# Two one-bank tiles in place of one two-bank tile for the transposes of an attention kernel, and own output banks for the MoE behind it

## Chip, cores and metric

One core of a Trainium2 chip runs the whole program. The metric is the device time of one execution, in microseconds, and its median over several runs. The profile shows one execution more. PE is TensorE (PEld its weight loads), ACT is ScalarE, DVE is VectorE, POOL is GpSimd, and SP issues most of the DMAs.

## What is computed

Attention over 4 batches of 8 heads, 576 positions and 64 values each, with a bias made by a small network from the log distance of two positions; then a feed-forward layer over the 2304 tokens, whose activation is a ratio of two polynomials ("MoE" in the code, though it has one expert). All is fp32.

```python
# attention
scores = q @ k.T / sqrt(64)
x = log1p(|i - j|) / log1p(max(i, 1))
scores += (relu(x * w1 + b1) @ w2)[head]        # 32 hidden units
attn = exp(scores - max(scores)); attn /= sum(attn) + 1e-9
out = attn @ v
# feed-forward, x is out with the heads side by side: 2304 x 512
h = x @ w_in                                    # 512 -> 2048
P = a0 + a1*h + a2*h**2 + a3*h**3
Q = 1 + |b0|*|h| + |b1|*h**2
y = (P / (Q + 1e-6)) @ w_out                    # 2048 -> 512
```

## The kernel before

The program has three stages in one hand-written order (`manual_schedule`): each engine executes its instructions in the order in which the code emits them, and the framework adds the waits on semaphores between engines. What an instruction waits for follows from the tiles that it reads and writes.

PSUM has eight banks of 512 fp32 columns. Before the change they are four tiles of two banks for the whole program: `HB[0]`, `HB[1]`, `HB[2]` and `TP`.

**Tables** (lines 640 to 735). The bias network is evaluated for 36 groups of 16 rows, in a fixed order. ACT and DVE make the hidden units (ring tiles, lines 684 and 686), PE multiplies by w2 (line 711) into `pa`, one of the four PSUM tiles in turn, and ACT evacuates it with a scale (line 716). The result goes to DRAM, and the bias tiles of the first pair of heads are read back from there. The units of row group y+2 are emitted ahead of the evacuation of y. The first two attention steps, `start(0)` and `start(1)`, are emitted behind the third-last and the last group.

**Attention** (lines 544 to 638). A step is 128 queries of a pair of heads; there are 72 steps (`NS`), and a round `rnd(r)` handles the steps i = 2r and i+1, with 35 rounds in the loop and the rest in `start` and `finish`. The scores of the two heads (j = 0, 1) go to `hb(i, j) = HB[(2i + j) % 3]`. PE works on the two halves of its rows (partitions 0 to 63 and 64 to 127) side by side; `weave` emits one list of operations for each half, by estimated times. In a round:
- first weave: scores of step i (line 329), and the transposes of the probabilities of step i-2 (line 413): sixteen of 64 x 64, eight by each half of PE. Half r writes `TP[:, r]`, its own bank. Two or more further ones ("ends") go to a spare part of a score tile.
- `copy(1)`, then `copy(0)` (line 430): ACT copies the bank of a half into the SBUF tile `pt`. Between the two stands another ACT operation, in many rounds a pass over expert weights (line 154).
- `tails` (line 433): DVE copies the ends. `e_ttr` (line 341): DVE adds bias to scores and finds the row's minimum. `e_exp` (line 357): ACT takes the exponential.
- second weave: scores of step i+1 and transposes of step i-1 into the same `TP`; then `copy(1)` and `copy(0)` again, with an exponential between.
- products with v (line 466) of steps i-3 and i-2, into spare parts of score tiles, copied out by DVE (line 476).

Beside this, DVE, ACT and POOL split the feed-forward weights into a high and a low part (lines 119 to 187), one job in three of four rounds.

`finish` transposes the last two steps with `copy()` for both banks at once, and starts the first products of the MoE.

**MoE** (lines 754 to 943). Ten passes: five token tiles (384 or 512 tokens) times two halves of the hidden units. A step s is two blocks of 128 hidden units: `mm1` (line 307) into `HB[s % 2]`, the ratio on ACT and DVE (`rat0`, `rat1`, `dvu` to `dv4`, `pl1`), and two steps later `mm2` (line 850) into the output banks, up to four of 128 tokens, kept over the four steps of a pass. `OUT` names them: the two banks of `TP` and of `HB[2]`. In the step after a pass `evac` copies them out (ACT, line 866, in the first five passes) or adds them to the first half's (DVE, line 871).

Of the kernel before, what the change touches and what calls it, by code (L numbers as in the profile page):

```python
# [16 lines left out]
P = 128  # L17
# [19 lines left out]
def tile_attn_moe(  # L37
# [53 lines left out]
    npool = ctx.enter_context(tc.tile_pool(name="npool", bufs=2))  # L91
    nc.gpsimd.memset(npool.tile([P, 64], F32, tag="fill", name="fill2", bufs=1)[:, 0:8], 0.0)
    psum = ctx.enter_context(tc.tile_pool(name="psum", bufs=1, space=PSUM))
    HB = [psum.tile([P, 2, 512], F32, tag=f"h{i}", name=f"hb{i}") for i in range(3)]
    TP = psum.tile([P, 2, 512], F32, tag="tp", name="tp")
    wsc = {}
    U16 = mybir.dt.uint16
    FN = KD * P
# [123 lines left out]
    with tc.manual_schedule():  # L222
# [3 lines left out]
        with ExitStack() as actx:  # L226
            apool = actx.enter_context(tc.tile_pool(name="apool", bufs=1))
            qkp = actx.enter_context(tc.tile_pool(name="qkp", bufs=2))
            epool = actx.enter_context(tc.tile_pool(name="epool", bufs=3))
            vpool = actx.enter_context(tc.tile_pool(name="vpool", bufs=3))  # L230

            sums = [apool.tile([P, P], F32, tag=f"sum{i}", name=f"sum{i}") for i in range(4)]
            for t in sums:
# [171 lines left out]
            def e_tp(i, sp, us):  # L405
                t = pt[i] = epool.tile([P, 9, P], F32, tag="pt", name=f"pt{i}")
                pb = prob.pop(i)
                ps = TP.rearrange("p r (x s) -> p r x s", s=64)
                to = t[:, 0:8].rearrange("p x (r s) -> p r x s", r=2)

                def turn(r, out, src):
                    x = slice(64 * r, 64 * r + 64)
                    T.transpose(out, src[x, :], ident[x, x])  # L413

                def op(*args):
                    return 57, lambda: turn(*args)

                main, ends = [], []
                for r in range(2):
                    main.append([  # L420
                        op(r, ps[:, r, x], pb[:, (S + 64 if x % 2 == 0 else 0) + x // 2 * P:][:, :P])
                        for x in range(8)
                    ])
                    ends.append([op(r, sp[:, r, SH:SH + 64], pb[:, 512:512 + P])])
                    for u in us:
                        ends[r].append(op(r, sp[:, r, SH + 64:SH + P], sums[u % 4]))

                def copy(r=None):
                    x = slice(0, 2) if r is None else r
                    A.copy(out=to[:, x], in_=ps[:, x])  # L430

                def tails():
                    op = V.tensor_copy(
                        out=t[:, 8].rearrange("p (r s) -> p r s", r=2), in_=sp[:, :, SH:SH + 64]
                    )
                    for u in us:
                        n = nsum(u)
                        rt = epool.tile([10, P], F32, tag="rt", name=f"rt{u}", bufs=2)
                        rsum[u] = dpool.tile([n, P], F32, tag=f"rs{u}", name=f"rs{u}")
                        V.tensor_copy(  # L440
                            out=rt[0:n].rearrange("p (r s) -> p r s", r=2), in_=sp[0:n, :, SH + 64:SH + P]
                        )
                        nc.sync.dma_start(out=rsum[u], in_=rt[0:n])
                    return op

                return main, ends, copy, tails
# [169 lines left out]
            def finish():  # L616
                run(puts)
                main, ends, copy, tails = turned(NS - 2, HB[2], ())
                weave(*(main[r] + ends[r] for r in range(2)))
                copy()  # L620
                tails()
                mm1(0, 0)
                recip(NS - 1)
                run(norms)
                main, ends, copy, tails = turned(NS - 1, HB[1], (NS - 1,))
                weave(*(main[r] + ends[r] for r in range(2)))
                copy()
                put = [e_pv(NS - 3, HB[2][:, 0, 0:P]), e_pv(NS - 2, HB[2][:, 1, 0:P])]
                put.pop(0)()
                tails()  # L630
                mm1(0, 1)
                put.pop(0)()
                put = e_pv(NS - 1, HB[2][:, 0, 0:P])
                done_to(NS)
                run(norms)
                load_rb(NU - 1)
                load_x(1, 1, KD - 1, KD)
                put()

            with ExitStack() as bctx:  # L640
# [21 lines left out]
                        out=lts[:, a:z], in0=lts[:, a:z], scalar1=w1s, scalar2=None, op0=ALU.mult  # L662
                    )
                for x in range(9):
                    T.matmul(TP[:, 0, 0:P], ident, ident, start=True, stop=True)  # L665

                def dist(n):
                    return max(NROW * n + NROW, S - NROW * n)
# [28 lines left out]
                for y, n in enumerate(order):  # L697
                    if y == 13:
                        load_v(1)
                    if y + LEAD < NG:  # L700
                        relu(order[y + LEAD])
                    i0 = NROW * n
                    mid = i0 + NROW - 1
                    pa = HB[2] if y == NG - 2 else TP if y == NG - 1 else (HB + [TP])[(y + 2) % 4]
                    cuts = sorted({0, mid, 512, EW})
                    for a, z in zip(cuts, cuts[1:]):
                        o = pa[:, a // 512, a % 512:a % 512 + z - a]
                        for c in range(4):
                            x = rows[n, c]
                            x = x[:, a - mid:z - mid] if a >= mid else x[:, mid - a:mid - z:-1]  # L710
                            T.matmul(  # L711
                                o[32 * c:32 * c + 32], w28[:, 32 * c:32 * c + 32], x,
                                start=True, stop=True,
                            )
                    e = rpool.tile([P, EW], F32, tag="e", name=f"e{n}")
                    A.activation(  # L716
                        out=e, in_=pa.rearrange("p a s -> p (a s)")[:, :EW], func=AF.Identity,
                        scale=rts[:, n:n + 1],
                    )
                    g, k = divmod(n, 8)  # L720
                    x0 = S - NROW - i0
                    nc.sync.dma_start(
                        out=tab[g][NROW * k:NROW * k + NROW, :, x0:x0 + EW].rearrange("r h x -> (r h) x"),
                        in_=e,
                    )
                    if y in done:
                        load_bias(0, done[y])
                    if y == NG - 1:
                        load_bias(0, 3)
                        load_bias(0, 4)  # L730
                    if y == NG - 3:
                        start(0)
                    if y == NG - 1:
                        start(1)
# [19 lines left out]
        with ExitStack() as mctx:  # L754
# [1 line left out]
            xb = bpool.tile([P, 10 * S], F32R, tag="bias", name="xb")  # L756
            n = KD * TM
            xps.append([xb[:, i * n:(i + 1) * n].rearrange("p (k t) -> p k t", k=KD) for i in range(2)])
            OUT = [TP[:, 0, :], TP[:, 1, :], HB[2][:, 0, :], HB[2][:, 1, :]]
            gg, po, rt = {}, {}, {}  # L760

            def et(s, nm, bufs, dt=F32):
# [66 lines left out]
            def mm2(s):  # L829
                n, fp = divmod(s, FPR)  # L830
                hi, lo = gg.pop(s)
                first, last = fp == 0, fp == FPR - 1
                todo = []
                nc_ = TS[n % NTT] // P
                for c in range(nc_):
                    if first:
                        po[n, c] = OUT[c]
                    for j in range(2):
                        todo += [(c, j, hi, woh), (c, j, hi, wol), (c, j, lo, woh)]
                if not last:  # L840
                    todo.sort(key=lambda x: x[2] is lo)
                elif s == NQ - 1:
                    todo.sort(key=lambda x: (x[0] // 2, x[2] is lo))
                for c in range(nc_):
                    mine = [x for x in todo if x[0] == c]
                    po[n, c, "ends"] = (mine[0], mine[-1])
                for x in todo:
                    c, j, l, r = x
                    a, z = po[n, c, "ends"]
                    T.matmul(  # L850
                        po[n, c], l[:, j, c * P:(c + 1) * P], r[fp][:, j, :],
                        start=(first and x is a), stop=(last and x is z),
                    )
                    if last and x is z:
                        evq.append((n, c))
# [40 lines left out]
            for s in range(NQ + LAG + 1):  # L896
                def at(d):
                    return 0 <= s - d < NQ
# [10 lines left out]
                if n > NTT:  # L909
                    evac(late)  # L910
                    late = []
                if at(1):
                    rat1(s - 1)
                evac(late)
                if at(LAG):
                    mm2(s - LAG)
                if at(1):
                    dv2(s - 1)
                    dv3(s - 1)
                    dv4(s - 1)  # L920
                if at(0):
                    rat0(s)
                    job(s, 2)
# [98 lines left out]
```

## Time and profile before

| | us |
|---|---|
| median of 3 runs | 759.36 |
| lowest and highest | 757.29, 760.0 |
| the profiled execution | 758.72 |
| its span, first to last instruction | 756.6 |
| PE busy | 707.8 (94%) |
| DVE busy | 557.6 (74%) |
| ACT busy | 477.1 (63%) |
| POOL busy | 155.0 (20%) |

A busy share is an average over the three stages. Matmuls overlap in PE's pipeline and their ends are modelled, so a busy PE is not PE at its peak. The granted clock is a share of 2.4 GHz; the records hold 1.0 and 0.5 only, and a mean lies between.

### The profile page before, as it was taken

The page shows a single profiled execution, that of the slowest core. Times are in us where ns is not written, and L with a number is a line of the kernel's source. Part 1 is how long each engine was busy: PE and PEld are TensorE (multiplying, and loading weights), DVE is VectorE, ACT ScalarE, POOL GpSimd, SP SyncE. Part 2 cuts the span into 40 slices and gives each one's busy share as a digit, 9 for nine tenths or more (in the row PEclk, how much of TensorE's full clock was granted, in tenths as well). Part 3 has the DMA queues.
Part 4 walks back from the last instruction along what each step waited for, and adds up shares of the span by engine and source line. Part 5 has one row for each costly group of instructions (what it writes and reads, how often), then busy time and mean ns, then how long its engine had stood idle before and what let it go on. Part 6 is the DMA issues. An engine that isn't in the chain of part 4 may idle for free.

```text
span 756.6 us, 16077 instructions
## 1 busy us (share of the span) xinstructions
PE 707.8 (94%) x6274; PEld 594.0 (79%) x6274; DVE 557.6 (74%) x1012; ACT 477.1 (63%) x791; POOL 155.0 (20%) x122
## 2 busy tenths in 40 slices
PE   9978888888888888898999999999999999999998
PEld 6657777677777777778988888889998888888896
DVE  8964656554666565664899989898887887888776
ACT  7966656665676575676677565665665665556542
POOL 0000122232223132110122212222112122212210
PEclk9999989998999898899999999999999999999999
DMA  7887384466548764512444626176765130303021
GB/s 249 294 287 259 116 250 151 153 195 203 170 148 243 229 209 162 180 49 75 156 157 126 223 67 225 57 260 199 238 219 184 42 112 0 140 15 111 1 98 42
DMA packets 74843, 118.96 MB, mean 157 GB/s; under 512 B 11904, under 2 KB 33808, under 8 KB 74768
## 3 DMA queue, kind: packets, MB, share of 16 engines
q1 hardware_dynamic: 74624, 117.79, 47.2%
q8 instruction: 49, 0.80, 0.4%
q14 instruction: 26, 0.21, 0.1%
q10 hardware_dynamic: 144, 0.16, 0.1%
HBM read 79.17 MB, written 35.61 MB: 152 GB/s over the span
## 4 chain that ended last, share of the span: by engine, by line
PE 89%; ACT 6%; DVE 2%; issue 2%; DMA 1%; POOL 0%; SPq 0%; ACTq 0%; DVEq 0%; POOLq 0%
PE hb L307 26%; PE tp L850 14%; PE hb L466 13%; PE hb L850 12%; PE hb L329 8%; PE tp L413 8%; PE hb L711 4%; ACT pt L430 3%; PE hb L413 2%; ACT wh L154 2%; PE tp L711 1%; DVE s L341 1%; DMA tab<-e 1%; PE tp L665 1%; DVE wm L170 0%
## 5 line engine op out<-in xcount | busy, mean ns | idle before, releaser
L341 DVE CUSTOM_DVE_ANT_0 s<-hb,bias 128x576 f32<-128x576 f32 x144 | 104.0, 755 | 87.7 <-PE hb L329 67.0
L430 ACT COPY pt<-tp 128x512 f32<-128x512 f32 (+1 forms) x142 | 82.3, 588 | 107.5 <-PE hb L329 85.1
L820 POOL TENSOR_TENSOR gl<-m,r 128x1024 fp32r<-128x1024 f32 (+1 forms) x39 | 85.5, 2193 | 303.8 <-DVE m L813 258.2
L413 PEld LDWEIGHTS tp<-ident,p 64*128 64x128 f32 x1152 | 90.6, 144 | 65.1 <-ACT pt L430 56.3
L413 PE MATMUL tp<-ident,p 64*128 64x64 f32 x1152 | 102.7, 232 | 40.2 <-ACT pt L430 40.2
L329 PE MATMUL hb<-k,q 64*128 64x288 f32 (+1 forms) x640 | 134.2, 440 | 1.5 <-ACT e L716 1.5
L357 ACT ACTIVATE p<-s,m 128x576 f32<-128x576 f32 x144 | 111.7, 779 | 3.2 <-DVE m L341 3.2
L773 ACT ACTIVATE w<-hb,babs 128x1024 f32<-128x1024 f32 (+1 forms) x40 | 41.3, 1031 | 107.5 <-PE hb L307 107.5
L466 PE MATMUL hb<-pt,v 128*64 128x128 f32 (+1 forms) x1600 | 104.7, 296 | 0.4 <-DVE m L341 0.4
L466 PEld LDWEIGHTS hb<-pt,v 128*64 128x64 f32 x1600 | 95.9, 159 | 6.8 <-issue 3.1
L329 PEld LDWEIGHTS hb<-k,q 64*128 64x128 f32 (+1 forms) x640 | 74.7, 183 | 4.8 <-ACT e L716 1.6
L783 DVE SCALAR_TENSOR_TENSOR u<-w,babs,hb 128x1024 f32<-128x1024 f32 (+1 forms) x40 | 46.9, 1172 | 37.9 <-ACT t L774 37.8
L307 PE MATMUL hb<-xb,wih 128*128 128x512 f32 (+1 forms) x240 | 68.8, 367 | 0.0
L778 ACT ACTIVATE u<-u 128x1024 f32<-128x1024 f32 (+1 forms) x40 | 39.1, 977 | 40.6 <-DVE u L783 40.4
L799 DVE SCALAR_TENSOR_TENSOR gh<-t,cst,r 128x1024 fp32r<-128x1024 f32 (+1 forms) x40 | 46.9, 1174 | 9.3 <-ACT r L780 6.9
L806 DVE SCALAR_TENSOR_TENSOR m<-u,qc,gh 128x1024 f32<-128x1024 f32 (+1 forms) x40 | 47.1, 1178 | 4.4 <-DVE gh L799 0.5
L307 PEld LDWEIGHTS hb<-xb,wih 128*128 128x128 f32 x240 | 44.5, 188 | 6.1
L476 DVE COPY xs<-hb 128x128 f32<-128x128 f32 (+1 forms) x80 | 21.5, 276 | 36.2 <-PE hb L466 29.8
L813 DVE SCALAR_TENSOR_TENSOR m<-t,cst,m 128x1024 f32<-128x1024 f32 (+1 forms) x40 | 47.1, 1178 | 1.4
L792 DVE SCALAR_TENSOR_TENSOR t<-t,cst,hb 128x1024 f32<-128x1024 f32 (+1 forms) x40 | 47.0, 1174 | 1.4
L850 PE MATMUL tp<-wol,gh 128*128 128x512 f32 x120 | 46.9, 391 | 0.0
L850 PE MATMUL tp<-woh,gh 128*128 128x512 f32 x120 | 46.8, 390 | 0.0
(96 smaller groups left out, 1448.2 us busy)
## 6 DMA issues: line engine op xcount, KB each, us to landing
tab<-e SPq DMA_DIRECT2D x36, 295.5 KB
wx<-in_w_in_dram SPq DMA_DIRECT2D x16, 512.0 KB
wx<-in_w_out_dram SPq DMA_DIRECT2D x16, 512.0 KB
v<-in_vp_dram SPq DMA_DIRECT2D x16, 320.0 KB
ws<-wh SPq DMA_DIRECT2D x20, 256.0 KB
ws<-wl SPq DMA_DIRECT2D x20, 256.0 KB
q<-in_qt_dram SPq DMA_DIRECT2D x16, 288.0 KB
k<-in_kt_dram SPq DMA_DIRECT2D x16, 288.0 KB
```

Of the source, the lines that this page charges most:

```text
L307: T.matmul(hps[s][:, j, :w_], w[:, k, sl], x[:, k, :w_], start=(k == 0 and z == 0), stop=(k == KD - 1 and z == 2),)
L329: T.matmul(hb(i, j)[o, a, :SH], q[r, x], k[r, a * SH:(a + 1) * SH], start=True, stop=True,)
L341: V.tensor_tensor_reduce(out=t.rearrange("p (a s) -> p a s", a=2), in0=hb(i, j)[:, :, :SH], in1=bias[p][:, 5 * j + c, :].rearrange("p (a s ...
L357: A.activation(out=prob[i][:, z * S:z * S + S], in_=t, func=AF.Exp, bias=m, scale=-1.0, accum_out=sums[u % 4][:, k:k + 1],)
L413: T.transpose(out, src[x, :], ident[x, x])
L430: A.copy(out=to[:, x], in_=ps[:, x])
L466: T.matmul(ps[y, o], vt[n][:, kc, y], t[:, 2 * kc + j if kc < 4 else 8, o], start=(kc == 0), stop=(kc == 4),)
L792: V.scalar_tensor_tensor(out=rt[s, "t"], in0=rt[s, "t"], scalar=abs_[:, 1:2], in1=hp(s), op0=ALU.add, op1=ALU.mult,)
L806: V.scalar_tensor_tensor(out=m, in0=rt[s, "u"], scalar=qc, in1=rt[s, "gh"].bitcast(F32), op0=ALU.add, op1=ALU.mult,)
L813: V.scalar_tensor_tensor(out=m, in0=rt[s, "t"], scalar=abs_[:, 0:1], in1=m, op0=ALU.add, op1=ALU.subtract)
L820: eng.tensor_tensor(out=lo, in0=rt[s, "m"], in1=rt[s, "r0"], op=ALU.mult)
L850: T.matmul(po[n, c], l[:, j, c * P:(c + 1) * P], r[fp][:, j, :], start=(first and x is a), stop=(last and x is z),)
```

## The change

`TP` becomes a list of two tiles of one bank each, one for each half of PE's rows, and `copy(r)` copies one of them. `finish` copies half 1 and half 0 instead of both at once. These two tiles and `HB[2]` live in a pool of the attention (`ps_a`) that is given back at its end. The MoE takes its output banks from a pool of its own (`ps_o`), four tiles of one bank, each drawn anew for each pass. In the tables, three two-bank tiles rotate, and only the second-last group uses `TP`, with two evacuations (512 and 79 columns); the last one uses `HB[2]`. In the MoE's loop, `rat1` and the late `evac` are emitted behind `mm2`.

```diff
--- before.py
+++ after.py
@@ -91,8 +91,7 @@
     npool = ctx.enter_context(tc.tile_pool(name="npool", bufs=2))
     nc.gpsimd.memset(npool.tile([P, 64], F32, tag="fill", name="fill2", bufs=1)[:, 0:8], 0.0)
     psum = ctx.enter_context(tc.tile_pool(name="psum", bufs=1, space=PSUM))
-    HB = [psum.tile([P, 2, 512], F32, tag=f"h{i}", name=f"hb{i}") for i in range(3)]
-    TP = psum.tile([P, 2, 512], F32, tag="tp", name="tp")
+    HB = [psum.tile([P, 2, 512], F32, tag=f"h{i}", name=f"hb{i}") for i in range(2)]
     wsc = {}
     U16 = mybir.dt.uint16
     FN = KD * P
@@ -228,6 +227,9 @@
             qkp = actx.enter_context(tc.tile_pool(name="qkp", bufs=2))
             epool = actx.enter_context(tc.tile_pool(name="epool", bufs=3))
             vpool = actx.enter_context(tc.tile_pool(name="vpool", bufs=3))
+            ps_a = actx.enter_context(tc.tile_pool(name="ps_a", bufs=1, space=PSUM))
+            HB.append(ps_a.tile([P, 2, 512], F32, tag="h2", name="hb2"))
+            TP = [ps_a.tile([P, 512], F32, tag=f"tp{r}", name=f"tp{r}") for r in range(2)]
 
             sums = [apool.tile([P, P], F32, tag=f"sum{i}", name=f"sum{i}") for i in range(4)]
             for t in sums:
@@ -405,7 +407,7 @@
             def e_tp(i, sp, us):
                 t = pt[i] = epool.tile([P, 9, P], F32, tag="pt", name=f"pt{i}")
                 pb = prob.pop(i)
-                ps = TP.rearrange("p r (x s) -> p r x s", s=64)
+                ps = [x.rearrange("p (x s) -> p x s", s=64) for x in TP]
                 to = t[:, 0:8].rearrange("p x (r s) -> p r x s", r=2)
 
                 def turn(r, out, src):
@@ -418,16 +420,15 @@
                 main, ends = [], []
                 for r in range(2):
                     main.append([
-                        op(r, ps[:, r, x], pb[:, (S + 64 if x % 2 == 0 else 0) + x // 2 * P:][:, :P])
+                        op(r, ps[r][:, x], pb[:, (S + 64 if x % 2 == 0 else 0) + x // 2 * P:][:, :P])
                         for x in range(8)
                     ])
                     ends.append([op(r, sp[:, r, SH:SH + 64], pb[:, 512:512 + P])])
                     for u in us:
                         ends[r].append(op(r, sp[:, r, SH + 64:SH + P], sums[u % 4]))
 
-                def copy(r=None):
-                    x = slice(0, 2) if r is None else r
-                    A.copy(out=to[:, x], in_=ps[:, x])
+                def copy(r):
+                    A.copy(out=to[:, r], in_=ps[r])
 
                 def tails():
                     op = V.tensor_copy(
@@ -617,14 +618,16 @@
                 run(puts)
                 main, ends, copy, tails = turned(NS - 2, HB[2], ())
                 weave(*(main[r] + ends[r] for r in range(2)))
-                copy()
+                copy(1)
+                copy(0)
                 tails()
                 mm1(0, 0)
                 recip(NS - 1)
                 run(norms)
                 main, ends, copy, tails = turned(NS - 1, HB[1], (NS - 1,))
                 weave(*(main[r] + ends[r] for r in range(2)))
-                copy()
+                copy(1)
+                copy(0)
                 put = [e_pv(NS - 3, HB[2][:, 0, 0:P]), e_pv(NS - 2, HB[2][:, 1, 0:P])]
                 put.pop(0)()
                 tails()
@@ -662,7 +665,7 @@
                         out=lts[:, a:z], in0=lts[:, a:z], scalar1=w1s, scalar2=None, op0=ALU.mult
                     )
                 for x in range(9):
-                    T.matmul(TP[:, 0, 0:P], ident, ident, start=True, stop=True)
+                    T.matmul(TP[0][:, 0:P], ident, ident, start=True, stop=True)
 
                 def dist(n):
                     return max(NROW * n + NROW, S - NROW * n)
@@ -701,10 +704,14 @@
                         relu(order[y + LEAD])
                     i0 = NROW * n
                     mid = i0 + NROW - 1
-                    pa = HB[2] if y == NG - 2 else TP if y == NG - 1 else (HB + [TP])[(y + 2) % 4]
+                    if y == NG - 2:
+                        whole, pa = None, TP
+                    else:
+                        whole = HB[2 if y == NG - 1 else (y + 2) % 3]
+                        pa = [whole[:, 0], whole[:, 1]]
                     cuts = sorted({0, mid, 512, EW})
                     for a, z in zip(cuts, cuts[1:]):
-                        o = pa[:, a // 512, a % 512:a % 512 + z - a]
+                        o = pa[a // 512][:, a % 512:a % 512 + z - a]
                         for c in range(4):
                             x = rows[n, c]
                             x = x[:, a - mid:z - mid] if a >= mid else x[:, mid - a:mid - z:-1]
@@ -713,10 +720,12 @@
                                 start=True, stop=True,
                             )
                     e = rpool.tile([P, EW], F32, tag="e", name=f"e{n}")
-                    A.activation(
-                        out=e, in_=pa.rearrange("p a s -> p (a s)")[:, :EW], func=AF.Identity,
-                        scale=rts[:, n:n + 1],
-                    )
+                    if whole is None:
+                        parts = [(TP[0], 0, 512), (TP[1][:, :EW - 512], 512, EW)]
+                    else:
+                        parts = [(whole.rearrange("p a s -> p (a s)")[:, :EW], 0, EW)]
+                    for x, a, z in parts:
+                        A.activation(out=e[:, a:z], in_=x, func=AF.Identity, scale=rts[:, n:n + 1])
                     g, k = divmod(n, 8)
                     x0 = S - NROW - i0
                     nc.sync.dma_start(
@@ -756,7 +765,7 @@
             xb = bpool.tile([P, 10 * S], F32R, tag="bias", name="xb")
             n = KD * TM
             xps.append([xb[:, i * n:(i + 1) * n].rearrange("p (k t) -> p k t", k=KD) for i in range(2)])
-            OUT = [TP[:, 0, :], TP[:, 1, :], HB[2][:, 0, :], HB[2][:, 1, :]]
+            ps_o = mctx.enter_context(tc.tile_pool(name="ps_o", bufs=1, space=PSUM, reuse_waits="tile"))
             gg, po, rt = {}, {}, {}
 
             def et(s, nm, bufs, dt=F32):
@@ -834,7 +843,7 @@
                 nc_ = TS[n % NTT] // P
                 for c in range(nc_):
                     if first:
-                        po[n, c] = OUT[c]
+                        po[n, c] = ps_o.tile([P, DM], F32, tag=f"o{c}", name=f"o{n}_{c}", bufs=1)
                     for j in range(2):
                         todo += [(c, j, hi, woh), (c, j, hi, wol), (c, j, lo, woh)]
                 if not last:
@@ -909,15 +918,14 @@
                 if n > NTT:
                     evac(late)
                     late = []
-                if at(1):
-                    rat1(s - 1)
-                evac(late)
                 if at(LAG):
                     mm2(s - LAG)
                 if at(1):
+                    rat1(s - 1)
                     dv2(s - 1)
                     dv3(s - 1)
                     dv4(s - 1)
+                evac(late)
                 if at(0):
                     rat0(s)
                     job(s, 2)
```

## Rows read from the trace of the kernel before

**Rows 1.** Busy time by stage: stretch, its length, busy us (instructions), PEclk, DMA share, GB/s.
```profile
0.00:52.00 52.00, 47.55 (x898) 31.83 (x898) 45.13 (x123) 43.49 (x75) 1.63 (x15) 1.00 0.83 290
52.00:357.00 305.00, 264.30 (x3508) 224.34 (x3510) 177.62 (x542) 197.49 (x451) 67.82 (x68) 0.91 0.55 175
357.00:756.60 399.60, 395.90 (x1872) 337.88 (x1868) 334.82 (x349) 236.09 (x267) 85.55 (x39) 1.00 0.38 126
```
**Rows 2.** Waits of PE: who waited for whom: us in total, times, longest.
```profile
PE tp L413 <- ACT pt L430: 40.2, 35, 1.4
```
**Rows 3.** Waits of PE's weight loads.
```profile
PEld tp L413 <- ACT pt L430: 56.3, 35, 1.9
```
**Rows 4.** Timeline of ACT in one round: start, us, line, operation [idle before <-releaser].
```profile
203.62 0.58 ACT L430 COPY pt<-tp 128x512 f32<-128x512 f32 x1 [2.32 <-PE hb L329]
204.10 0.72 ACT L154 ACTIVATE wh<-wk,wmin 128x512 uint32<-128x512 uint32 x1
204.73 0.57 ACT L430 COPY pt<-tp 128x512 f32<-128x512 f32 x1
...
209.77 0.77 ACT L357 ACTIVATE p<-s,m 128x576 f32<-128x576 f32 x1
```
**Rows 5.** Timeline of PE in the same round.
```profile
202.06 0.29 PE L413 MATMUL tp<-ident,p 64*128 64x64 f32 x2
...
203.08 0.35 PE L413 MATMUL tp<-ident,p 64*128 64x64 f32 x3
203.27 0.70 PE L329 MATMUL hb<-k,q 64*128 64x288 f32 x2
205.36 0.65 PE L413 MATMUL tp<-ident,p 64*128 64x64 f32 x7 [1.38 <-ACT pt L430]
...
206.38 0.28 PE L413 MATMUL tp<-ident,p 64*128 64x64 f32 x2
...
207.08 2.40 PE L466 MATMUL hb<-pt,v 128*64 128x128 f32 x40
209.42 0.27 PE L413 MATMUL hb<-ident,p 64*128 64x64 f32 x1
```
**Rows 6.** Timeline of DVE at the end of that round.
```profile
208.93 0.31 DVE L433 COPY pt<-hb 128x128 f32<-128x128 f32 x1
```
**Rows 7.** Sum over the attention's thirteen stretches at half clock.
```profile
sum 54.59, PE 54.53 PEld 48.87 DVE 29.11 ACT 33.42 POOL 0.00; mean PE 4.19 PEld 3.76 DVE 2.24 ACT 2.57 POOL 0.00
```
**Rows 8.** Sum and mean over the 4 us ahead of each of the thirteen.
```profile
sum 52.00, PE 36.45 PEld 26.50 DVE 24.02 ACT 31.42 POOL 26.79; mean PE 2.80 PEld 2.04 DVE 1.85 ACT 2.42 POOL 2.06
```
**Rows 9.** The same stretches, the transposes (line 413) alone.
```profile
sum 52.00, PE 20.87 PEld 18.00; mean PE 1.61 PEld 1.38
```
**Rows 10.** Timeline of ACT in the tables.
```profile
23.55 1.17 ACT L684 ACTIVATE ring<-lts,bts 128x384 f32<-128x384 f32 x2
24.56 1.45 ACT L716 ACTIVATE e<-hb,cst 128x591 f32<-128x591 f32 x2
```
**Rows 11.** Timeline of ACT at the end of the tables.
```profile
48.41 0.73 ACT L716 ACTIVATE e<-hb,cst 128x591 f32<-128x591 f32 x1
49.05 0.74 ACT L716 ACTIVATE e<-tp,cst 128x591 f32<-128x591 f32 x1
```
**Rows 12.** Timeline of PE there.
```profile
49.20 1.24 PE L329 MATMUL hb<-k,q 64*128 64x288 f32 x8 [1.46 <-ACT e L716]
```
**Rows 13.** The copies of the attention by shape: count, busy us, mean ns, idle before.
```profile
L430 ACT COPY pt<-tp 128x512 f32<-128x512 f32 x140 | 80.3, 582 | 105.7 <-PE hb L329 85.1 <-PE tp L413 19.5 <-PE hb L413 1.2
...
L430 ACT COPY pt<-tp 128x1024 f32<-128x1024 f32 x2 | 2.0, 1010 | 1.8 <-PE tp L413 1.8
```
**Rows 14.** Timeline of ACT at the end of the MoE's first pass.
```profile
406.46 1.05 ACT L866 COPY os<-tp 128x512 f32<-128x512 f32 x2
```
**Rows 15.** Timeline of PE there.
```profile
408.00 0.39 PE L850 MATMUL tp<-woh,gh 128*128 128x512 f32 x1
```

## The prediction

> **What bounds the kernel now.** I read the busy time of the three stages first. In the last stage, the MoE, PE is busy 395.90 of 399.60 us at clock 1.00; in the first, the tables, 47.55 of 52.00. In the middle stage, the attention from 52 to 357 us, PE is busy 264.30 of 305.00 us at a mean granted clock of 0.91, ACT 197.49 and DVE 177.62 [rows 1]. So PE sets the pace everywhere, and only in the attention does it lose time. Second, the waits of PE: one kind makes nearly all of that loss, the transposes (line 413) that wait for the copies out of their tile (line 430), 40.2 us in 35 waits [rows 2]; the same stop seen on the weight loads is 56.3 us [rows 3]. The loop has 35 rounds, so it is one wait a round. Third, the timeline of one round, to see which wait it is [rows 4, 5].
>
> In the round at 201.6 us the first weave's eight transposes of half 1 have ended at 202.35 us (202.06 + 0.29), those of half 0 at 203.43 (203.08 + 0.35) [rows 5]. The copy of half 1 starts at 203.62, 0.19 after the last transpose of the *other* half, with ACT idle for 2.32 us before it; the weight pass (line 154) follows at 204.10 and the copy of half 0 at 204.73, ending at 205.30 [rows 4]. PE is through with what it can do at 203.97 (203.27 + 0.70) and takes up the second weave's half-1 transposes at 205.36, 0.06 after the copy of half 0, although the half that they overwrite was out by 204.20 [rows 4, 5]. Both directions thus wait for the whole two-bank tile and not for the half concerned. This is what the change can undo.
>
> **The change, part by part.** *Two tiles instead of one.* The same round by the same durations: copy 1 may start at 202.35 + 0.19 = 202.54, since ACT is free from 201.30, and ends at 203.12. The weight pass starts 0.48 later, at 203.02, and the next copy 0.63 after that, at 203.65 (its own transposes release it at 203.62); it ends at 204.22. The second weave's half-1 transposes need only copy 1: at 203.97 it has been done for 0.85 us. Its half-0 transposes come 1.02 us after those (206.38 against 205.36), at 204.99, and find copy 0 done for 0.77 us. The stop of 1.39 us becomes nothing. It is covered with 0.8 us to spare on both sides.
>
> Over all rounds the saving lies between the 40.2 us of PE's idle time and the 56.3 us of the weight loads' [rows 2, 3]. The first counts from the modelled end of the last product, the second from the last load, so PE could have issued somewhere between. I take 45, nearer the PE row, since matmuls are what must end.
>
> *Where the stop goes.* What follows the second weave moves up with it: the scores' reductions on DVE, the products with v (207.08, 2.40 us), the next round at 209.42 [rows 5]. DVE's copy of the transposes' ends (208.93 + 0.31 = 209.24) must be done before the next round's first score product at 209.42, which writes the same bank: 0.18 us to spare [rows 6]. It follows PE's second weave by DVE's own work, so it moves up by as much, until DVE has no idle time left: 177.62 us of work in then some 240 is three quarters. ACT: the last exponential of the round ends at 210.54 (209.77 + 0.77) [rows 4]; moved up as PE, it delays the next copy 1 by about 0.2 us against the end of its transposes (209.42 + 0.71 + 0.19 = 210.32), inside the 0.85. I charge 4 us for rounds where DVE or ACT is later than in this one; bounds 0 and 35 x 0.4 = 14.
>
> *The clock.* Thirteen stretches of the attention ran at half clock (1.2 of 2.4 GHz), 54.59 us together, PE busy for 54.53 of them [rows 7]. At full clock half of that, 27.3 us, would not have been spent. In the 4 us ahead of each of the thirteen PE was busy for a mean of 2.80 us only [rows 8], of which 1.61 us hold transposes [rows 9]: they are the stretches with the two weaves and the stop between them. With the stop gone, a stretch of 4 us always holds more products. I take 20 of the 27.3 us back; bounds 0 and 27.3.
>
> The Trainium skill speaks against this (TensorE: Matmul & The Clock Gate, Part 4, PE-mode transpose): it says that transposes don't count as busy time for the clock gate. By it the weaves would go on looking quiet, and the clock's share would stay near 0.91; the first rival below is priced for that, from rows. The trace bears the rule out in part: what stands ahead of the falls is rich in transposes.
>
> *The tables.* Three banks of two rotate instead of four. A row's ring tiles made by ACT stand in ACT's order behind the evacuation three rows back (two ring tiles, then evacuations, [rows 10]), so those rows never could start earlier; the rows of DVE alone find the third-last one read. Nothing, below 1 us. But the last row now goes to HB[2], and the second attention step's first product writes HB[2] too. Before, it waited 1.46 us for the evacuation at 48.41, ending at 49.14, and started at 49.20 [rows 11, 12]; now it waits for the one at 49.05, ending at 49.79, and the evacuation of the row ahead, split in two, costs ACT some 0.15 more. That is 0.65 + 0.15 = +0.8 us, and it delays the whole attention. Bounds 0.5 and 1.2.
>
> *Finish.* Two copies of 1024 columns (1010 ns) become four of 512 (582 ns each) [rows 13]: 2 x 0.15 us on ACT, beneath the MoE's first products; if bare, 0.3.
>
> *MoE.* The order on each engine's queue stays: ACT still does rat1, then the evacuations; dv2 to dv4 are DVE's, mm2 is PE's. Each output bank is now released alone. At the first tile's end the evacuations of banks 0 and 1 start at 406.46 and end at 407.51, and PE comes at 408.00 [rows 14, 15]; PE waits for none of them now, so a finer release gains nothing. If a bank were released only with the last of its tile, it would be some 0.2 us late at nine tile ends: at most 2 us. I take 0.
>
> **Sum.** 758.7 (the profiled execution) + 0.8 - 45 + 4 - 20 = 698.5 us. The median of the runs shown is 0.6 above that execution, so 699.
>
> **Rivals.** (1) *The clock's share stays.* The stop goes, but the weaves are still what the clock falls behind. Attention of 305 - 41 = 264 us would hold 54.6 x 264/305 = 47.3 us at half clock: 3.7 us back instead of 20. Time 699 + 16 = 715. For it: the transposes' share ahead of the falls [rows 9]; against it: 1.2 us of idle PE time in 4 as well [rows 8].
> (2) *Another engine takes over.* DVE's or ACT's order makes the scores' banks late in most rounds, and half of the 45 us comes back: 699 + 22 = 721, and with some clock lost again 725. For it: the 0.18 us at the round's end [rows 6]; against it: ACT is idle 105.7 us before these copies [rows 13].
> (3) *The wait is not the shared tile.* Then only the table's 0.8 us is left: 760. Against it: the idle ACT and the 0.06 us between copy 0's end and PE's start.
> (4) *Slower: the clock falls more often.* Denser weaves without pauses might leave whole rounds at half clock. Each us at half clock costs half a us, so the 40 us gained are gone once about 80 us more than now, some 135 of 264, run at half clock; all of the attention there would give over 800. Nothing speaks for it but the transposes' share; the MoE's dense stretches run at 1.00 [rows 1].
> (5) *All of it:* 56.3 and 27.3 us and no new wait: 758.7 + 0.8 - 83.6 = 676.
>
> **How the numbers follow.** Forecast (about 688 to 710) 0.59, rival 1 (710 to 720) 0.18, rival 2 (720 to 735) 0.11, rival 5 (below 688) 0.06, rival 3 0.03, rival 4 0.03. A difference within 0.5%, 3.8 us, is what a measurement can't tell from none. So faster 0.94, same 0.03, slower 0.03. From 680 to 728 holds all but a part of rivals 2 and 5 and the last two.
>
> **What would show it.** The row of line 413 waiting for line 430 falls from 40.2 us to below 5. Copy 1 stands in front of the first weave's last transposes. PE busy in the attention near 95% of its stage, the stage near 245 us instead of 305, mean clock there above 0.95 (0.91 says rival 1). PE waits for DVE's copies of ends or sums at a round's start say rival 2. The MoE still takes 395 to 400 us at clock 1.00. The first product at the second step starts near 50.0 instead of 49.20. I am wrong if the wait row stays, or if it moves to another bank.

## The result and the profile after

The changed kernel takes 702.80 us (median of 4 runs, 697.17 to 702.94) against 758.33 us for the kernel before (756.17 to 760.00). The ratio is 0.9248, with a 95% interval of 0.9206 to 0.9289: 7.5% faster. The forecast was 699, in a range of 680 to 728. The profiled execution is the fastest of the four, 697.17 us with a span of 695.0; the other three lie at 702.7 to 702.9 with a mean clock of 0.978 instead of 0.983, and two more executions on record took 699.39 and 701.83 us. Medians are of all executions of a kernel, while ratios set its executions in the fast state against those of the kernel before in the same session. What follows is counted between profiled executions: 697.17 - 758.72 = -61.55 us.

Lines have shifted: the transposes are line 415 (413 before), the copies 431 (430), the scores 331 (329), the products with v 467 (466), the exponential 359 (357), the table's evacuation 728 (716), the copy of the products into the `xs` tiles 477 (476).

The stages after, cut at the first transpose and at the end of the attention, answer [rows 1]: stretch, its length, busy us (instructions) of PE, PEld, DVE, ACT and POOL, PEclk, DMA share, GB/s.

```profile
0.00:53.10 53.10, 47.77 (x900) 32.98 (x901) 45.12 (x123) 43.84 (x77) 1.64 (x15) 1.00 0.81 284
53.10:295.50 242.40, 230.50 (x3508) 202.73 (x3510) 175.78 (x540) 196.42 (x452) 67.83 (x68) 0.95 0.69 220
295.50:695.00 399.50, 395.89 (x1872) 337.88 (x1868) 334.89 (x349) 236.44 (x268) 85.67 (x39) 1.00 0.38 126
```

All of the gain lies in the attention, 242.40 us instead of 305.00. PE is busy for 95% of it (it was 87%), at clock 0.95 (0.91), with the same 3508 matmuls. The MoE has 399.50 us (399.60). The tables are 1.1 us longer.

The waits of PE after answer [rows 2]: who waited for whom, us in total, times, longest.

```profile
PE hb L331 <- DVE xs L477: 11.2, 5, 4.0
PE hb L331 <- ACT e L728: 2.2, 1, 2.2
PE hb L415 <- DVE m L343: 1.6, 1, 1.6
```

The waits of the weight loads after answer [rows 3].

```profile
PEld tp L415 <- ACT pt L431: 2.2, 5, 0.4
```

The row of 40.2 us in 35 waits is gone altogether, and the weight loads' row has fallen from 56.3 to 2.2 us. In its place stands a wait that before did not have: five times a score product of a round, behind the round's first ones, waits for DVE's copy of the products with v into an `xs` tile, 11.2 us.

One round on ACT and on PE after, to be held beside [rows 4] and [rows 5]: start, us, line, operation [idle before <-releaser].

```profile
202.14 0.59 ACT L431 COPY pt<-tp 128x512 f32<-128x512 f32 x1 [0.47 <-PE hb L415]
203.11 0.59 ACT L431 COPY pt<-tp 128x512 f32<-128x512 f32 x1 [0.39 <-PE hb L331]
203.59 0.78 ACT L359 ACTIVATE p<-s,m 128x576 f32<-128x576 f32 x1
```
```profile
201.03 0.28 PE L415 MATMUL hb<-ident,p 64*128 64x64 f32 x1
...
202.63 0.35 PE L415 MATMUL tp<-ident,p 64*128 64x64 f32 x3
202.82 0.46 PE L331 MATMUL hb<-k,q 64*128 64x288 f32 x1
202.82 0.47 PE L415 MATMUL tp<-ident,p 64*128 64x64 f32 x5
...
206.95 0.27 PE L415 MATMUL hb<-ident,p 64*128 64x64 f32 x1
```

The copy of half 1 runs from 202.14 to 202.73, before the last transposes of half 0 (202.63 + 0.35 = 202.98), which it used to follow. The second weave's half-1 transposes start at 202.82, about 0.1 us behind it, and no stop stands between the weaves. They start together with a score product of the other half of PE's rows. The round lasts 206.95 - 201.03 = 5.92 us.

The stretches of the attention at half clock after answer [rows 7]; the columns are those of the stages.

```profile
53.23:56.64 3.41, 3.41 (x34) 3.22 (x33) 1.29 (x4) 1.72 (x6) 0.00 (x0) 0.50 0.75 217
121.50:124.91 3.41, 3.41 (x34) 3.29 (x31) 1.58 (x7) 2.62 (x7) 1.24 (x2) 0.50 0.80 247
179.52:186.35 6.83, 6.51 (x50) 5.05 (x52) 3.10 (x9) 2.96 (x7) 1.79 (x2) 0.50 0.23 63
240.96:251.20 10.24, 7.78 (x62) 6.31 (x64) 4.70 (x12) 4.23 (x10) 3.07 (x3) 0.50 0.33 106
sum 23.89, PE 21.11 PEld 17.87 DVE 10.67 ACT 11.53 POOL 6.10; mean PE 5.28 PEld 4.47 DVE 2.67 ACT 2.88 POOL 1.52
```

Four stretches are left of thirteen, and PE is busy in them for 21.11 us instead of 54.53: 27.3 - 21.11 / 2 = 16.7 us came back. The first lies behind the longer idle time at the attention's start. The other three lie behind or around three of PE's new waits, which end at 119.99, 179.84 and 243.42 us.

The longest of the new waits, first in the chain of waits (start, us, what), then as DVE and as PE show it.

```profile
237.41 5.54 DMA xd<-xs
...
243.07 0.30 DVE xs L477
...
243.42 1.70 PE hb L331 x9
```
```profile
243.07 0.29 DVE L477 COPY xs<-hb 128x128 f32<-128x128 f32 x1 [5.06 <-DMA xd<-xs]
```
```profile
243.42 2.18 PE L331 MATMUL hb<-k,q 64*64 64x288 f32 x12 [3.96 <-DVE xs L477]
```

The tile's scaling on POOL, SP's issues behind it, and the DMA share while the store was under way (a window, columns as above):

```profile
234.40 0.80 POOL L394 TENSOR_TENSOR xs<-xs,rb 128x288 f32<-128x288 f32 x1
```
```profile
234.53 2.40 SPq L219 DMA_DIRECT2D wg<-ws  x4
237.03 0.29 SPq L444 DMA_DIRECT2D rs<-rt  x1
237.41 0.33 SPq L396 DMA_DIRECT2D xd<-xs  x1
```
```profile
237.41:242.95 5.54, 2.05 (x26) 1.24 (x21) 0.61 (x3) 2.49 (x6) 0.00 (x0) 0.82 0.89 298
```

An `xs` tile collects a unit's results from the products with v. POOL scales it and a transfer on SP's queue stores it to `xd`; there are three such tiles. POOL was through at 235.20, but SP issued five other transfers from 234.53 on and the store only at 237.41; it landed 5.54 us later, with the DMA engines busy for 0.89 of that time. DVE's copy into the reused tile stood still until then, and the bank that it reads is one that PE's next scores write. In the kernel before, DVE waited for these stores once, for 0.7 us; after, in five waits, 15.5 us.

### The profile page after: what moved, and what is told of

It is laid out like the page before. It is cut to its first block, busy times and chain, and to the rows that moved or that the text cites. A ratio compares the mean times of both kernels' runs of the same rounds, so it can differ in the third digit from the quotient of the medians.

```text
span 695.0 us, 16103 instructions
## 1 busy us (share of the span) xinstructions
PE 674.2 (97%) x6274; PEld 573.6 (83%) x6274; DVE 555.8 (80%) x1012; ACT 476.7 (69%) x794; POOL 155.1 (22%) x122
## 4 chain that ended last, share of the span: by engine, by line
PE 92%; DMA 4%; DVE 2%; POOL 1%; issue 1%; ACT 0%; SPq 0%; DVEq 0%; POOLq 0%; ACTq 0%
PE hb L309 28%; PE o L859 28%; PE hb L467 10%; PE hb L331 10%; PE tp L415 7%; PE hb L718 6%; DMA xd<-xs 3%; PE hb L415 2%; DVE s L343 1%; PE tp L668 1%; DMA k<-in_kt_dram 0%; DVE xs L477 0%; POOL wm L165 0%; POOL xs L394 0%; ACT e L728 0%
## 5 line engine op out<-in xcount | busy, mean ns | idle before, releaser
L331 PE MATMUL hb<-k,q 64*128 64x288 f32 (+1 forms) x640 | 129.9, 450 | 13.7 <-DVE xs L477 11.2
L343 DVE CUSTOM_DVE_ANT_0 s<-hb,bias 128x576 f32<-128x576 f32 x144 | 103.8, 756 | 31.7 <-PE hb L331 19.3
L431 ACT COPY pt<-tp 128x512 f32<-128x512 f32 x144 | 83.7, 582 | 45.9 <-PE tp L415 21.9
L415 PEld LDWEIGHTS tp<-ident,p 64*128 64x128 f32 x1152 | 88.5, 144 | 10.4 <-issue 5.0
L415 PE MATMUL tp<-ident,p 64*128 64x64 f32 x1152 | 96.5, 232 | 0.0
L467 PE MATMUL hb<-pt,v 128*64 128x128 f32 (+1 forms) x1600 | 88.3, 266 | 0.4 <-DVE m L343 0.4
L859 PE MATMUL o<-wol,gh 128*128 128x512 f32 x216 | 84.2, 390 | 0.0
L859 PE MATMUL o<-woh,gh 128*128 128x512 f32 x216 | 84.2, 390 | 0.0
L467 PEld LDWEIGHTS hb<-pt,v 128*64 128x64 f32 x1600 | 79.8, 138 | 3.3 <-DVE m L343 0.6
L859 PE MATMUL o<-woh,gl 128*128 128x512 f32 x216 | 53.8, 389 | 0.0
```

Of the source, the lines that this page charges most:

```text
L331: T.matmul(hb(i, j)[o, a, :SH], q[r, x], k[r, a * SH:(a + 1) * SH], start=True, stop=True,)
L343: V.tensor_tensor_reduce(out=t.rearrange("p (a s) -> p a s", a=2), in0=hb(i, j)[:, :, :SH], in1=bias[p][:, 5 * j + c, :].rearrange("p (a s ...
L431: A.copy(out=to[:, r], in_=ps[r])
L467: T.matmul(ps[y, o], vt[n][:, kc, y], t[:, 2 * kc + j if kc < 4 else 8, o], start=(kc == 0), stop=(kc == 4),)
L859: T.matmul(po[n, c], l[:, j, c * P:(c + 1) * P], r[fp][:, j, :], start=(first and x is a), stop=(last and x is z),)
```

## The experiments

**Swap the order of the copies.** Of the changed kernel, `rnd` alone is edited: both weaves copy half 0 first, then half 1. The halves are still two tiles.

```
 weave(ends[0] + sc[0] + main[0], main[1] + ends[1] + sc[1])
-copy(1)
+copy(0)
...
-copy(0)
+copy(1)
...
 weave(sc[0] + main[0] + ends[0], main[1] + sc[1] + ends[1])
-copy(1)
-e_exp(i, 1)
 copy(0)
+e_exp(i, 1)
+copy(1)
```

> The changed kernel with half 0 copied ahead of half 1 in both weaves of a round. Theory (the gain comes from half 1 being copied while half 0 is still transposed): half 0 is the later one, so its copy holds half 1's behind it in ACT's order, and the second weave's half-1 transposes wait for it again: 35 waits of PE for line 431 of about 1.2 us, 40 us in all, and a time of 740 to 758. Rival (any two separate tiles do, whatever the order of the copies): no such wait, 697 to 703.

Measured: 758.68 us (median of 10 runs, 751.04 to 763.98), ratio 0.9973 (0.9921 to 1.0025). The wait of PE, and one round on ACT and on PE:

```profile
PE tp L415 <- ACT pt L431: 40.1, 35, 1.4
```
```profile
200.25 0.58 ACT L431 COPY pt<-tp 128x512 f32<-128x512 f32 x1 [1.75 <-PE hb L331]
200.74 0.72 ACT L153 ACTIVATE wh<-wk,wmin 128x512 uint32<-128x512 uint32 x1
201.36 0.57 ACT L431 COPY pt<-tp 128x512 f32<-128x512 f32 x1
```
```profile
201.99 0.65 PE L415 MATMUL tp<-ident,p 64*128 64x64 f32 x7 [1.39 <-ACT pt L431]
```

The time lies just above the 740 to 758 that were expected, and the 35 stops are back, to a tenth of a us in all. With half 0 first, ACT waits for the last transposes of the weave, and half 1, which the second weave needs first, is copied last: PE resumes 0.06 us after its end (201.36 + 0.57 = 201.93). Two tiles by themselves are worth nothing; they are worth all of it once the half that is ready first, and wanted first, is copied first.

**The attention's part alone.** Into the kernel before go the two one-bank tiles, their separate copies and the tables' rotation of three; the MoE keeps its four output banks and its loop order.

```
-TP = psum.tile([P, 2, 512], F32, tag="tp", name="tp")
+TP = [psum.tile([P, 512], F32, tag=f"tp{r}", name=f"tp{r}") for r in range(2)]
...
-def copy(r=None):
-    x = slice(0, 2) if r is None else r
-    A.copy(out=to[:, x], in_=ps[:, x])
+def copy(r):
+    A.copy(out=to[:, r], in_=ps[r])
...
-OUT = [TP[:, 0, :], TP[:, 1, :], HB[2][:, 0, :], HB[2][:, 1, :]]
+OUT = [TP[0], TP[1], HB[2][:, 0, :], HB[2][:, 1, :]]
```

> The kernel before with the two one-bank tiles, the separate copies and the three rotating tiles of the tables; the MoE's output banks and its order stay as before. Theory (all of the gain is the attention's): 697 to 703, the MoE stage 395 to 400 us. Rival (the MoE's own output banks give part of it): above 706.

Measured: 701.95 us (median of 4, 699.84 to 703.38), ratio 0.9263 (0.9211 to 0.9316), the same as the whole change within its interval. The MoE stage, cut behind the attention's last transposes, and the new wait, which is there too:

```profile
299.70:699.20 399.50, 395.84 (x1872) 337.94 (x1868) 334.88 (x349) 236.15 (x268) 86.19 (x40) 1.00 0.37 126
```
```profile
PE hb L329 <- DVE xs L475: 14.8, 5, 4.6
```

**One tile of two banks, all else changed.** The changed kernel gets its two halves as views of one tile; pools, tables and the MoE's banks stay as changed.

```
-TP = [ps_a.tile([P, 512], F32, tag=f"tp{r}", name=f"tp{r}") for r in range(2)]
+TT = ps_a.tile([P, 2, 512], F32, tag="tp", name="tp")
+TP = [TT[:, 0], TT[:, 1]]
```

> The changed kernel, with the two halves' banks in one two-bank tile again; the copies stay separate, the pools, the MoE's own output banks and the tables stay as changed. Theory: the waits of PE for line 431 come back, 35 of them, about 40 us, and the time is 755 to 762. Rival (the pools or the MoE's banks carry part of the gain): under 750.

Measured: 760.36 us (median of 10, 754.46 to 767.39), ratio 1.0033 (0.9987 to 1.0078).

```profile
PE tp L416 <- ACT pt L432: 39.6, 35, 1.4
...
PE hb L332 <- DVE xs L478: 2.1, 1, 2.1
```

Copies of one bank each, in the good order, but behind one shared tile: the stop is whole again. This and the run before it place the gain in the split of the tile, with the copies in the order that the kernel before had, and nothing in the rest of the change. One wait of 2.1 us for an `xs` tile is left here too.

**A fourth `xs` tile.** If the new waits are those for a tile whose store has not landed, one more tile takes them away, and with them the falls of the clock behind them.

```
-xs[x] = npool.tile([P, S], F32, tag="xs", name=f"xs{x}", bufs=3)
+xs[x] = npool.tile([P, S], F32, tag="xs", name=f"xs{x}", bufs=4)
```

> The changed kernel with four xs tiles instead of three. After the change PE waits five times, 11.2 us in all, for DVE's copies into xs, which wait for the store of an older xs. Theory A (those waits come from the number of xs tiles, and the clock falls because of them): the waits are gone, less than 12 us at half clock in the attention instead of 23.9, time 682 to 690. Theory B (the waits go, but the clock falls as often, since the weaves cause it): 688 to 693, half clock near 24 us. Theory C (the DMAs are late whatever the number of tiles): the wait turns up at another place, 697 to 703.

Measured: 677.82 us (median of 4, 676.92 to 678.10), ratio 0.8945 (0.8897 to 0.8992). The waits of PE, then the windows of the stretch at half clock at the attention's start and of the attention behind it:

```profile
PE hb L331 <- ACT e L728: 2.3, 1, 2.3
PE hb L415 <- DVE m L343: 1.6, 1, 1.6
```
```profile
51.40:58.23 6.83, 5.21 (x43) 4.60 (x43) 3.27 (x9) 3.90 (x10) 0.00 (x0) 0.50 0.50 163
58.30:276.20 217.90, 217.49 (x3470) 192.14 (x3468) 173.43 (x535) 192.56 (x443) 67.83 (x68) 1.00 0.75 241
```

No `xs` wait is left, and behind 58.3 us the attention runs at clock 1.00 with PE busy for 217.49 of 217.90 us. Between the profiled executions the tile gave 697.17 - 677.84 = 19.3 us: 11.2 of waits, and of the clock (21.11 - 4.97) / 2 = 8.1, since of the half clock only the 4.97 us between the first transpose, at 53.26, and 58.23 are left. This is more than the 682 to 690 that were expected for theory A: the clock came back as well, wholly but for the start. Between the medians it is 25.0 us.

**The last table group into the transposes' banks.** On top of the fourth tile, the last group of table rows goes to the two transpose banks and the one ahead of it to HB[2], the order that the kernel before had.

```
-if y == NG - 2:
+if y == NG - 1:
     whole, pa = None, TP
 else:
-    whole = HB[2 if y == NG - 1 else (y + 2) % 3]
+    whole = HB[2 if y == NG - 2 else (y + 2) % 3]
```

> Four xs tiles, and the tables' last group evacuated from the two one-bank tiles again, the second-last from HB[2], as in the kernel before. Theory (the later first product of the second attention step, and the idle PE ahead of it, cost about 1 us and the one half-clock stretch of 6.8 us that is left in the attention): that product starts near 49.3 us instead of 50.34, 3.4 us or none at half clock there, time 672 to 676.5. Rival (it is hidden behind the wait for DVE's minimum): 677 to 678.5.

Measured: 674.45 us (median of 4, 674.38 to 676.89), ratio 0.8889 (0.8861 to 0.8917), the best version here. The second step's first product starts a microsecond earlier than in the run before (50.34 there):

```profile
49.33 1.24 PE L331 MATMUL hb<-k,q 64*128 64x288 f32 x8 [1.46 <-ACT e L728]
```

The profiled execution, 676.89 us, is 0.95 us below the run before and still has a stretch of 6.8 us at half clock at the start of the attention, where 3.4 or none was expected:

```profile
50.98:57.82 6.84, 5.62 (x48) 5.25 (x50) 3.19 (x10) 4.55 (x11) 0.00 (x0) 0.50 0.53 169
```

The other three, 674.4, show a mean clock of 0.999 over the whole span. So about 1 us is the wait, and what lies beyond that came with the clock at the start; which idle time there decides on it was not tried.

**The fourth tile in the kernel before.** The `bufs=4` of the run with the fourth tile, on the kernel before and alone.

```
-xs[x] = npool.tile([P, S], F32, tag="xs", name=f"xs{x}", bufs=3)
+xs[x] = npool.tile([P, S], F32, tag="xs", name=f"xs{x}", bufs=4)
```

> The kernel before with four xs tiles and nothing else. Theory (the store of xs became late only because the rounds became shorter): no difference, 755 to 760. Rival (the number of xs tiles cost the kernel before as well): 745 or less.

Measured: 755.43 us (median of 10, 747.45 to 759.96) against 760.13 (752.93 to 762.06) for the kernel before in the same session, ratio 0.9929 (0.9889 to 0.9968). The stop is as it was:

```profile
PE tp L413 <- ACT pt L430: 39.6, 35, 1.4
```

The tile that is worth 25 us behind the change is worth some 5 ahead of it, 2 to 8 by the interval: little, though not clearly nothing, and the kernel before itself has medians of 757.31 to 760.13 in the three sessions. The wait for the stores is, for the most part, one that the faster attention made: before, PE has none; the slow kernel with one tile for both halves has one, of 2.1 us; after, there are five, 11.2 us.

## Why the prediction was right, and where its sizes were off

**The cause: right.** Both directions of the stop were the shared tile. Joining the halves again brings it back whole (39.6 us in 35 waits), swapping the copies does the same (40.1), and the attention's part alone gives the whole gain. Rival 3 (the wait is not the shared tile) is out, and so is rival 4: the clock rose.

**The stop: 57 us, not 45.** The run with four `xs` tiles has neither stop nor new wait, so it prices the stop. Against the kernel before it is 758.72 - 677.84 = 80.9 us shorter, 82.0 with the 1.14 us by which its attention starts later (50.34 against 49.20 in [rows 12]). The clock accounts for 27.3 - 4.97 / 2 = 24.8 of these; 57.2 remain. That is the row of the weight loads, 56.3 us [rows 3], not PE's 40.2 [rows 2]. The step that was off is "nearer the PE row, since matmuls are what must end". In the round worked out there PE was to take up the second weave's transposes at 203.97, 2.3 us behind the round's start at 201.64, when the two score products at 203.27 have ended; in the round shown above it does so 1.79 us behind (202.82 - 201.03). Those two products already belong to the second weave, by its code, and run on the other half of PE's rows. After the change the first of them starts at 202.82, together with the transposes, so their end was never what the transposes had to wait for. Copy 1 has only 0.09 us to spare in this round for the same reason (202.82 - 202.73, where the prediction had 0.85): the transposes come 0.54 us earlier in the round than was worked out, and the copy ends 0.22 later. The Trainium skill names a further reason why the end is a poor mark (Perfetto Trace Analysis, Tensor Engine Instruction): the profiler works a matmul's end out from the instruction's size and does not observe it. No run here tells how much of the 16 us between the two rows comes from that. By the ends the stop was 40 us, by the loads 56, and taking it away gave 57.

**New waits: 11.2 us, not 4.** The prediction looked for the stop's successor at the round's start, in DVE's copy of the transposes' ends with 0.18 us to spare [rows 6]. The row at 209.42 from which that was counted is one of transposes; the round's first score product, which writes the copied bank, came later, so that 0.48 us were to spare (209.72 - 209.24):

```profile
209.72 0.46 PE L329 MATMUL hb<-k,q 64*128 64x288 f32 x1
```

After the change PE has no wait for that copy. What was late next is a chain that it did not follow: `xs` tile, POOL, store, tile again. Its pace hangs on SP's order and on the transfer's own time: 2.21 us from POOL's end to the store's issue and 5.54 to its landing, in the longest case. 11.2 lies inside the bounds of 0 to 14, but by luck: those were made for another wait. The sign "if it moves to another bank" came true for this part of the stop.

**The clock: 16.7 us back, not 20.** The direction was right. What is missing follows the new waits: with these gone, nothing but the start runs at half clock. So the rest of the 27.3 us was not the weaves', and rival 1 fails on its mechanism as well. The transposes alone (busy time of PE and PEld), in the stretch without falls of the run with four `xs` tiles:

```profile
58.30:276.20 217.90, 96.39 (x1302) 88.54 (x1301) 1.00 0.75 241
```

They fill 1.77 us of each 4 there (96.39 / 217.90 x 4), more than the 1.61 ahead of the falls [rows 9], which the prediction called rich in transposes. What those ahead of the falls had more of is idle time: PE was busy for 2.80 us of 4 [rows 8], against 3.47 on average (264.30 / 305 x 4). By the Trainium skill's rule (TensorE: Matmul & The Clock Gate, Part 4, PE-mode transpose), on which rival 1 stood, the dense weaves would still look quiet; 218 us at clock 1.00 with the same transposes speak against that reading of this kernel. No run here has the transposes without the products between them, so whether they count by themselves stays open.

**The start: 1.02 us, not 0.8.** The second step's first product came at 50.22 instead of 49.20, in the bounds of 0.5 to 1.2; putting the last group back won 1.0.

**At nothing: right.** The MoE is 0.1 us shorter, and the run without its part of the change gives the same time, 399.50 us for its MoE stage too.

**The sum.** +1.0 - 57.2 + 11.2 - 16.7 = -61.7 us, with -61.55 measured between the profiled executions. That the forecast of -60.2 came so near is luck in its sizes: 12 us too little for the stop stood against 7 too little for the new waits and 3 too much for the clock. This account is that of the fastest execution; against the median of 702.80 the forecast of 699 was 3.8 us too low. The 5.6 us between the two are not taken apart here; the attention's part alone, profiled at 701.36, has 14.8 us of waits instead of 11.2. Rival 2, another engine taking over, happened in small: 11 us of waits and 8 of clock, on a DMA's account, in 5 rounds rather than in most. Rival 5, 676 us with no new wait, is what the fourth tile then gave: 677.8.

## What to carry to other kernels

Where an engine stands idle beside work that should be ready, compare the copy's start with the last write to the *whole* tile, not to the part that it reads; split the tile so that each part is released alone, and copy first the part that the next stage overwrites first. When a stop is taken out of a loop, follow each ring of buffers whose pace is not the loop's own, its stores above all, since these can become the next stop, as they did here, and a further buffer may cost nothing. Price a stop of PE by its weight loads as well as by the ends of its products, and take the clock that falls behind it into the account.

## What the runs showed of the hardware that was not expected

Short stops that recur cost clock as well as their own time: before, 35 stops of at most 1.4 us on PE's row, 40.2 us in all, went with 54.6 us at half clock, 27.3 us lost; with no stop, matmuls of the same kinds ran for 218 us at clock 1.00. Fewer and longer stops cost about as much for their length: five waits of 11.2 us went with 20.5 us at half clock, 8.9 us lost ((21.11 - 3.41) / 2). A single stop of 4.0 us, at 243.4, had 10.2 us at half clock around it.

A store of 288 KB took 5.54 us from its issue to its landing in a stretch with the DMA engines busy for 0.89 of it. The same transfers in a shorter attention load the DMA engines more: 0.69 of the stage instead of 0.55.
